# Second x chunk as plain rows, transposed on TensorE, and all of B in 128-row loads

## The chip, the cores and the metric

One core of a Trainium2 chip runs the kernel. The metric is the device time of one execution in microseconds (us), and lower is better. Every execution quoted here was classed as fast. "The profile" is the trace of one execution and the page made from it; its times are us from the start of the span. The span is some 1.8 us shorter than the device time of the same execution.

## The reference, cut to what matters

Only the first half of part A is touched by the change and by the argument: `Bu`, the product of x with two matrices B (real and imaginary part), ahead of a recurrence along the sequence.

```python
x: (1, 2048, 1024) bf16          B_re, B_im, C_re, C_im: (1024, 1024) bf16
Bu = einsum("bld,pd->blp", x, B_bar)          # contraction over d = 1024
for t in range(2048): h = Lam_bar * h + Bu[:, t, :]     # done in 8 chunks of 256
y = 2 * einsum("blp,dp->bld", hseq, Cmat).real + x * Dskip
out = g * y + (1 - g) * (x + an 8-row update of a gated MLP)
```

The kernel's matmuls contract over the partitions, so x and B are both needed transposed, with d on the partitions. Two chunks of x (512 rows) are worked on together: for each of eight channel tiles of 128 channels, 8 matmuls with B_re and 8 with B_im.

## The kernel before

The loads at the top, all on SyncE's queue but for one, and the opening of the work. `dma_start_transpose` loads and transposes in the DMA; `s1u` is one group of 8 matmuls (tile, B_re or B_im, chunks k0 to k1); `s1e` evicts a tile from PSUM on ScalarE; `warm` runs matmuls whose result nobody uses.

```python
x0r = const.tile([P, BPC, D], BF16, ...)                 # BPC = 2 tiles of 128 rows: chunk 0
for tl in range(BPC):
    (nc.scalar if tl else nc.sync).dma_start(x0r[:, tl, :], x2d[tl*P:(tl+1)*P, :])
load_B(0, 0, 1)                                          # B_re, channel tile 0, transposed
...                                                      # three tiny loads on ScalarE's queue
load_xT(1)                                               # chunk 1 of x, transposed, 256 rows
load_B(1, 0, 1)                                          # B_im, channel tile 0
for c0, c1 in ((1, 2), (2, 3), (3, 4), (4, 6), (6, 8)):
    for pl in range(2):
        load_B(pl, c0, c1)
load_X(1)                                                # chunks 2 and 3, then C, ...
...
warm(14)
for tl in range(BPC):                                    # chunk 0: 8 transposes a tile, then copies
    xq = ps_s2.tile([P, KD, P], BF16, name="xq", tag="zps")
    for dc in range(KD):
        nc.tensor.transpose(xq[:, dc, :], x0r[:, tl, dc*P:(dc+1)*P], ident[:])
    for h, copy in enumerate((nc.vector.tensor_copy, nc.scalar.copy)):
        copy(out=X[0][:, hs, tl*P:(tl+1)*P], in_=xq[:, hs, :])
warm(2)
...                                                      # tables: VectorE makes arguments, ScalarE sines
warm(1)
s1u(0, 0, 0, 0, 1)                                       # tile 0, B_re, chunk 0
warm(2)
s1u(0, 0, 0, 1, 2)                                       # tile 0, B_re, chunk 1
s1u(0, 0, 1, 0, 2)                                       # tile 0, B_im, both chunks
s1e(0, 0)
...                                                      # two tiny transposes (vb_ps), then
s1(0, 1)                                                 # tile 1: 16 matmuls of 512 columns
```

## Time and profile before

| | before |
|---|---|
| time, three timed runs | 247.49 us median (247.4 to 248.19) |
| span of the profiled execution | 246.1 us (device time 247.9) |
| TensorE busy | 240.6 us, 98% |
| VectorE, ScalarE busy | 92%, 48% |
| last wait of TensorE for a load | until 23.61 us |

Read it from the last row: TensorE is never without work after 23.61 us, so the end is fixed by when that stretch begins. The prediction shows the lines themselves.

### The profile page before, as it was taken

Reading aid. Unit: us, or ns where it says so; the run is one execution under the profiler, and the core shown is the slowest. Engines: PE = TensorE matmul, PEld = TensorE weight load, DVE = VectorE, ACT = ScalarE, POOL = GpSimd, SP = SyncE. Lnnn points to the kernel's source line nnn. Section 1 sums busy time; section 2 is a strip of 40 time slices with the busy share of each in tenths; the row PEclk is TensorE's granted clock in tenths of the full one; section 3 lists DMA queues with packets and bytes.
Section 4 is the critical chain, followed back from the end, with each engine's and each line's share of the span. In section 5 each row is a group of like instructions: output and inputs, shape, how many; then the busy total and the mean of one; then the engine's idle time right before and its main releaser. Section 6 shows DMA issues by size and latency. Waiting matters only on the chain.

```text
span 246.1 us, 3533 instructions
## 1 busy us (share of the span) xinstructions
PE 240.6 (98%) x1381; PEld 112.2 (46%) x1381; DVE 226.2 (92%) x230; ACT 119.3 (48%) x206; POOL 26.8 (11%) x47
## 2 busy tenths in 40 slices
PE   8998999999999999999999999999999999999994
PEld 5443444444444444444444444444444444446453
DVE  1799999999999999999999999999999999999932
ACT  3699973333462572223355462235267445456421
POOL 4000000000000301620002040100100211110210
PEclk9999999999999999999999999999999999999999
DMA  7899999999760450666257979778599999962052
GB/s 195 194 149 226 230 244 273 202 239 284 236 181 0 106 153 0 134 125 224 77 188 218 351 226 338 237 224 314 184 390 286 363 306 296 89 142 37 3 133 82
DMA packets 65313, 48.48 MB, mean 197 GB/s; under 512 B 50560, under 2 KB 52224, under 8 KB 65296
## 3 DMA queue, kind: packets, MB, share of 16 engines
q1 hardware_dynamic: 59968, 37.20, 58.1%
q0 software_dynamic: 3264, 7.38, 14.3%
q10 hardware_dynamic: 2064, 3.68, 4.1%
q8 instruction: 11, 0.18, 0.3%
q14 instruction: 6, 0.05, 0.1%
HBM read 27.55 MB, written 8.40 MB: 146 GB/s over the span
## 4 chain that ended last, share of the span: by engine, by line
PE 89%; SPq 7%; DMA 2%; issue 0%; DVE 0%
PE zps L767 42%; PE vps L271 39%; SPq L80 6%; PE zps L783 3%; PE pgu L659 3%; DMA BT<-in_A_B_im_dram 2%; PE y L671 1%; SPq L92 1%; PE zr L485 1%; DVE ot L788 0%; SPq L77 0%; PE xselT_ps L572 0%; PE zs_ps L588 0%; PE zt L492 0%; PE fl_ps L535 0%
## 5 line engine op out<-in xcount | busy, mean ns | idle before, releaser
L271 PE MATMUL vps<-X,BT 128*128 128x512 bf16 (+1 forms) x520 | 112.6, 376 | 1.2 <-DMA BT<-in_A_B_im_dram 0.9
L767 PE MATMUL zps<-CT,H 128*128 128x512 bf16 x480 | 105.0, 379 | 0.0
L271 PEld LDWEIGHTS <-BT 128*128 128x128 bf16 x520 | 50.1, 98 | 61.7 <-DMA BT<-in_A_B_im_dram 1.7
L767 PEld LDWEIGHTS <-H 128*128 128x128 bf16 x480 | 46.5, 98 | 56.6 <-issue 1.3
L278 ACT CAST V<-vps 128x512 bf16<-128x512 f32 x64 | 34.3, 588 | 58.6 <-PE vps L271 58.6
L308 DVE TENSOR_TENSOR_SCAN U<-d,U 128x2048 bf16<-128x2048 f32 (+2 forms) x22 | 62.0, 2860 | 0.6
L772 ACT ACTIVATE ot<-zps,gcol 128x512 bf16<-128x512 f32 x30 | 20.6, 686 | 46.3 <-PE zps L767 46.3
L741 ACT CAST zps<-xd 128x512 f32<-128x512 bf16 (+1 forms) x29 | 16.6, 576 | 3.6 <-ACT xt L728 3.3
L297 DVE TENSOR_TENSOR U<-V,T2tab 128x4096 bf16<-128x4096 bf16 (+2 forms) x11 | 16.6, 1511 | 0.7 <-ACT V L278 0.2
L298 DVE TENSOR_TENSOR V<-V,nTi 128x4096 bf16<-128x4096 bf16 (+2 forms) x11 | 16.7, 1516 | 0.5
L299 DVE TENSOR_TENSOR U<-U,V 128x4096 bf16<-128x4096 bf16 (+2 forms) x11 | 16.7, 1516 | 0.4
L793 POOL DMA_DIRECT2D out_dram<-ot x14 | 12.9, 923 | 32.5 <-ACT ot L772 30.4
L333 DVE TENSOR_TENSOR U<-U,S2tab 128x4096 bf16<-128x4096 bf16 x7 | 16.0, 2292 | 0.2
L335 DVE TENSOR_TENSOR H<-H,U 128x4096 bf16<-128x4096 bf16 x7 | 16.0, 2292 | 0.2
L728 ACT ACTIVATE xt<-xt,omgcol 128x1024 bf16<-128x1024 bf16 x14 | 16.0, 1144 | 0.0
L331 DVE TENSOR_TENSOR H<-U,Ctab 128x4096 bf16<-128x4096 bf16 x7 | 16.0, 2284 | 0.0
L705 POOL DMA_DIRECT2D xt<-in_A_x_dram x12 | 7.1, 594 | 80.9 <-DMA out_dram<-xt 42.9
L366 DVE TENSOR_TENSOR_SCAN U<-D,U 128x1024 bf16<-128x1024 f32 x4 | 8.9, 2279 | 0.1
L723 DVE TENSOR_TENSOR xd<-xt,Dbc 128x1024 bf16<-128x1024 bf16 x14 | 9.0, 683 | 0.0
L659 PE MATMUL pgu<-wgu,xsel 128*32 128x448 bf16 x128 | 7.2, 355 | 0.0
L783 PE MATMUL zps<-CT,H 128*128 128x256 bf16 (+1 forms) x48 | 7.1, 308 | 0.0
L718 POOL DMA_DIRECT2D out_dram<-xt x2 | 1.5, 752 | 49.2 <-DVE xt L717 49.2
(152 smaller groups left out, 127.6 us busy)
## 6 DMA issues: line engine op xcount, KB each, us to landing
wgu<-in_B_w_gate_dram SPq DMA_DIRECT2D x16, 448.0 KB, 3.5
wgu<-in_B_w_up_dram SPq DMA_DIRECT2D x16, 448.0 KB, 6.1
out_dram<-ot POOLq DMA_DIRECT2D x14, 256.0 KB, 6.0
wdb<-in_B_w_down_dram SPq DMA_DIRECT2D x7, 512.0 KB, 10.6
xt<-in_A_x_dram POOLq DMA_DIRECT2D x12, 256.0 KB, 4.3
out_dram<-xt ACTq DMA_DIRECT2D x12, 256.0 KB, 5.2
wd<-in_B_w_down_dram SPq DMA_DIRECT2D x5, 512.0 KB, 7.8
xt<-in_A_x_dram SPq DMA_DIRECT2D x4, 256.0 KB, 4.1
```

The lines of the kernel that those rows point to most:

```text
L271: nc.tensor.matmul(o, lhsT=BT[pl][:, dc, ct * P:(ct + 1) * P], rhs=X[m][:, dc, k0 * LC:k1 * LC], start=(dc == 0), stop=(dc == KD - 1))
L278: nc.scalar.copy(out=V[k][:, :, ct, :], in_=vp[m, ct][:, :, kk, :])
L297: nc.vector.tensor_tensor(out=u, in0=v, in1=T2tab[:, :, c0:c1, :], op=ALU.mult)
L298: nc.vector.tensor_tensor(out=v, in0=v, in1=bc(nTi, c0, c1), op=ALU.mult)
L299: nc.vector.tensor_tensor(out=u, in0=u, in1=V[k][:, ::-1, c0:c1, :], op=ALU.add)
L308: nc.vector.tensor_tensor_scan(out=fl, data0=d0[:, c0:c1, :].rearrange("p c t -> p (c t)"), data1=fl, initial=0.0, op0=ALU.mult, op1=ALU.add)
L331: nc.vector.tensor_tensor(out=h, in0=g, in1=bc(Ctab, c0, c1), op=ALU.mult)
L333: nc.vector.tensor_tensor(out=g, in0=g, in1=S2tab[:, :, c0:c1, :], op=ALU.mult)
L335: nc.vector.tensor_tensor(out=h, in0=h, in1=G[k][:, ::-1, c0:c1, :], op=ALU.add)
L741: nc.scalar.copy(out=z[:], in_=xd[b][:, d_:d_ + w])
L767: nc.tensor.matmul(zps[:], lhsT=H[k][:, pl, ct, tl * P:(tl + 1) * P], rhs=CT[pl][:, ct, dsl], start=(fresh and ct == 0 and pl == 0), stop= ...
L772: nc.scalar.activation(out=ots[b][:, dsl], in_=zps[:], func=ACT.Copy, scale=gcol[:, b:b + 1])
```

## The change

Its intent: take 2.6 us of issue out of SyncE's queue ahead of B by loading chunk 1 of x as plain rows and transposing it on TensorE, and let each tile of B come as early as it can by loading all of B in 128-row pieces. The helpers' new places are cut.

```diff
-    x0r = const.tile([P, BPC, D], BF16, name="x0r", tag="XP2")
+    x0r = const.tile([P, 2 * BPC, D], BF16, name="x0r", tag="XP2")
...
-    load_xT(1)
+    for tl in range(BPC, 2 * BPC):
+        nc.sync.dma_start(x0r[:, tl, :], x2d[tl * P:(tl + 1) * P, :])
     load_B(1, 0, 1)
-    for c0, c1 in ((1, 2), (2, 3), (3, 4), (4, 6), (6, 8)):
+    for c0, c1 in ((c, c + 1) for c in range(1, NCT)):
...
-        for h, copy in enumerate((nc.vector.tensor_copy, nc.scalar.copy)):
+        for h, copy in enumerate((nc.vector.tensor_copy if tl < BPC else nc.scalar.copy, nc.scalar.copy)):
...
+    warm(1)
+    s1u(0, 0, 0, 0, 1)
+    for tl in range(BPC, 2 * BPC):
+        x_tile(tl)
...
-    warm(1)
-    s1u(0, 0, 0, 0, 1)
-    warm(2)
-    s1u(0, 0, 0, 1, 2)
-    s1u(0, 0, 1, 0, 2)
+    s1u(0, 0, 1, 0, 1)
+    for pl in range(2):
+        s1u(0, 0, pl, 1, 2)
```

More of the change, by code (lines that the diff above doesn't have):

```diff
@@ L155, with x_tile @@
     vec = small.tile([P, 3, NCT], F32, name="vec")
-    for tl in range(BPC):
+    def x_tile(tl):
         xq = ps_s2.tile([P, KD, P], BF16, name="xq", tag="zps")
@@ L159 @@
             nc.tensor.transpose(xq[:, dc, :], x0r[:, tl, dc * P:(dc + 1) * P], ident[:])
-        for h, copy in enumerate((nc.vector.tensor_copy, nc.scalar.copy)):
+        for h, copy in enumerate((nc.vector.tensor_copy if tl < BPC else nc.scalar.copy, nc.scalar.copy)):
             hs = slice(h * KD // 2, (h + 1) * KD // 2)
             copy(out=X[0][:, hs, tl * P:(tl + 1) * P], in_=xq[:, hs, :])
+    for tl in range(BPC):
+        x_tile(tl)
     warm(2)
@@ L188, with s1u @@
     nc.scalar.activation(out=rdec[:], in_=are[:], func=ACT.Exp)
+    vp = {}
+    def s1u(m, ct, pl, k0, k1):
+        if (m, ct) not in vp:
+            vp[m, ct] = ps_s1.tile([P, 2, 2, LC], F32, name="vps", tag="vps")
+        o = vp[m, ct][:, pl, k0:k1, :].rearrange("p k t -> p (k t)")
+        for dc in range(KD):
+            nc.tensor.matmul(o, lhsT=BT[pl][:, dc, ct * P:(ct + 1) * P], rhs=X[m][:, dc, k0 * LC:k1 * LC], start=(dc == 0), stop=(dc == KD - 1))
+    warm(1)
+    s1u(0, 0, 0, 0, 1)
+    for tl in range(BPC, 2 * BPC):
+        x_tile(tl)
     Ctab = const.tile([P, NCT, LC], BF16, name="Ctab")
@@ L262 @@
     H = {}
-    vp = {}
-    def s1u(m, ct, pl, k0, k1):
-        if (m, ct) not in vp:
-            vp[m, ct] = ps_s1.tile([P, 2, 2, LC], F32, name="vps", tag="vps")
-        o = vp[m, ct][:, pl, k0:k1, :].rearrange("p k t -> p (k t)")
-        for dc in range(KD):
-            nc.tensor.matmul(o, lhsT=BT[pl][:, dc, ct * P:(ct + 1) * P], rhs=X[m][:, dc, k0 * LC:k1 * LC], start=(dc == 0), stop=(dc == KD - 1))
     def s1e(m, ct):
```

## The prediction

> **What bounds the kernel now.** I read the page's summary first, then the chain that ended last in order of time, then TensorE's waits, then the first 24 us engine by engine.
>
> ```profile
> PE 240.6 (98%) x1381; PEld 112.2 (46%) x1381; DVE 226.2 (92%) x230; ACT 119.3 (48%) x206; POOL 26.8 (11%) x47
> ...
> PE 89%; SPq 7%; DMA 2%; issue 0%; DVE 0%
> ```
>
> TensorE is busy for 98% of the span and makes up 89% of the chain; the other 9% (SyncE's issues and one transfer) is all ahead of 24 us. The chain, in order (start, length, what):
>
> ```profile
> 14.68 3.56 SPq L80
> 18.24 0.04 issue
> 18.29 5.27 DMA BT<-in_A_B_im_dram
> 23.56 0.05 issue
> 23.61 36.43 PE vps L271 x168
> ```
>
> The last thing TensorE waits for is the 256-row load of B_im for channel tiles 4 and 5, landed at 23.56. From 23.61 the chain is matmul after matmul to 242.9, so **the end is 23.61 plus a fixed 222.5 us**. Only what moves the matmuls at 23.61 can move the end. TensorE's own waits (total us, times, longest) say how much is lost there:
>
> ```profile
> PE vps L271 <- DMA BT<-in_A_B_im_dram: 0.9, 2, 0.7
> PE vps L271 <- DMA X<-in_A_x_dram: 0.2, 1, 0.2
> ```
>
> and its order of time (start, length, group) says where:
>
> ```profile
> 4.11 1.07 PE L159 MATMUL xq<-ident,x0r 128*128 128x128 bf16 x16
> ...
> 5.93 1.05 PE L271 MATMUL vps<-X,BT 128*128 128x256 bf16 x8
> 6.82 0.38 PE L152 MATMUL wps<-wt 128*128 128x256 bf16 x2
> 7.44 1.03 PE L271 MATMUL vps<-X,BT 128*128 128x256 bf16 x8 [0.24 <-DMA X<-in_A_x_dram]
> 8.65 1.90 PE L271 MATMUL vps<-X,BT 128*128 128x512 bf16 x8 [0.18 <-DMA BT<-in_A_B_im_dram]
> 10.48 0.20 PE L436 MATMUL vb_ps<-ident,vrow 8*128 8x8 bf16 x2
> 10.62 12.26 PE L271 MATMUL vps<-X,BT 128*128 128x512 bf16 x56
> 23.61 0.61 PE L271 MATMUL vps<-X,BT 128*128 128x512 bf16 x2 [0.73 <-DMA BT<-in_A_B_im_dram]
> ```
>
> The group at 10.62 is 56 matmuls (tiles 1, 2, 3 and half of 4) one every 0.216 us, without a hole; then 0.73 us of nothing. Two places can thus give time: the start of tile 1 (10.62) and the hole of 0.73.
>
> **What the Trainium skill says.** "TensorE: Matmul & The Clock Gate", Part 4 (PE-mode transpose): a TensorE transpose takes about 390 ns alone or 275 ns in one kernel, and its result lies in PSUM, so a copy has to follow. The trace agrees on the copy, but pipelined the 16 transposes stand one every 56 ns (1.07 us with the last one's latency). The same page, Part 1 (engine queue depths): ScalarE works strictly in order; ScalarE's row here does too, and my main doubt rests on it. "DMA: Bandwidth & Descriptors", "Issuing engines are not separate DMA queues": issue time is usually small beside the transfer. The trace disagrees for transposing loads: SyncE spends 1.31 us on 128 rows (256 KB) and 2.60 us on 256 rows, but 0.39 us on 128 plain rows. The same page, HWDGE ordering: each DMA engine takes descriptors in ring order, so the new rows stand behind B's first tile, not beside it.
>
> **The change part by part.**
>
> SyncE: the transposing load of x's second chunk (2.60 us of issue, 2.57 to 5.17) becomes two plain ones (2 x 0.39, plus 0.05 between issues, 0.88 in all). Every later issue is 1.76 us earlier. The four B loads of 256 rows become eight of 1.31: 0.0 to 0.2 more per pair than an unimpeded 2.60, so B_re tile 4 is issued at 14.68 - 1.76 = 12.92 and B_im tile 4 at 12.92 + 1.35 = 14.3, instead of in an instruction that ran from 18.29 to 20.71. With the 3.4 to 5.3 us that B loads took from issue to landing, it lands by 17.7 to 19.6; TensorE needs it near 23. **The hole of 0.73 goes**, with over 3 us to spare. Tiles 5, 6 and 7 follow at 2.7 us a pair against a need of 3.45 us a pair, and x's third and fourth chunks are still issued about 1.5 us earlier than before.
>
> TensorE: added are 16 transposes x 56 ns = 0.9 us, and the 8 matmuls of 512 columns become 16 of 256 (16 x 0.108 = 1.72 for 8 x 0.216 = 1.73: nothing). Removed are two warm-ups (0.2) and the waits 0.24 and 0.18. Step by step, as an estimate from these rows: B_re tile 0 lands at 5.9 as before, first half-group 5.93 to 6.79. Rows issued at 2.57 and 3.01 land near 6.3 and 6.8 (the transposed chunk, the same bytes in the same place, landed at 7.44 with its issue done only at 5.17). Transposes 6.79 to 7.69. B_im tile 0, issued at 3.45 in place of 5.21, lands near 7.9; its half-group runs 7.9 to 8.8. The other two half-groups need the copies.
>
> ScalarE: added are four copies, all in order. The same copies are in the trace before at 0.59 us latency and about 0.47 us from one start to the next. First one when the first eight transposes are done, 6.79 + 0.66 = 7.45 (the 0.66 is 4.11 to 4.77 before); starts 7.47, 7.94, 8.41, 8.88, end 9.46. TensorE starts chunk 1 when the third copy is done (9.0), its fifth matmul when the fourth is (9.5), so the two half-groups end at 9.95 and 10.8, two small transposes follow, and tile 1 starts at **10.95 against 10.62: 0.33 later**. From there 56 matmuls take 12.08: 23.03 in place of 23.61, a gain of **0.58 us**.
>
> The copies also push the table load behind them. Before:
>
> ```profile
> 6.94 1.28 ACT L223 ACT_TABLE_LOAD   x1
> 10.01 1.06 ACT L223 ACTIVATE nTi<-tf 128x1024 bf16<-128x1024 f32 x1 [1.78 <-DVE tf L212]
> ...
> 12.46 1.05 ACT L278 CAST V<-vps 128x512 bf16<-128x512 f32 x2
> ```
>
> Of the 1.78 us of slack, loading from 9.42 to 10.7 eats all and 0.7 more. ScalarE is without a gap from 10.01 to 25.4, so each eviction comes 0.7 later: tile 0 ends at 14.2, tile 1 (16.01 to 17.07 before) at 17.8. There are two accumulators, so tile 2 needs the first (TensorE is there at 14.40) and tile 3 the second (17.86). Both fit, with 0.2 and 0.1 us. I take off 0.08 for one of them missing: 0.5 us, **247.49 - 0.5 = 247.0**.
>
> **The rivals.** (1) *ScalarE takes over the wait.* The margins of 0.2 and 0.1 are thinner than my estimates of landings: rows or copies later by 0.4 make TensorE stop ahead of tile 2 or 3, each us of delay giving one us back. For it: the gapless ScalarE row. Against: it catches up before tile 5. It would give 247.2 to 247.6. (2) *The hole was all, and the start costs nothing*: rows land early, the ScalarE delay is small, tile 1 starts at 10.5: gain 0.8 to 1.0, 246.5. (3) *VectorE becomes the bound.* It is 92% busy and practically gapless from 6.4, and everything of it after the second table moves 0.7 later while TensorE comes 0.5 earlier. Against: its results are early; H of chunk 1 is done at 75.3 and used from 79.3, H of the last half-chunk at 232.2 and used from 235.8. A shift of 1.2 fits in 3.6, so no time. (4) *Smaller B loads starve TensorE*: 256 KB per 1.35 us is 194 GB/s against 512 KB per 3.45 us used, 152. Not unless a stall like that of the 3.56 us issue repeats, for which there are now 3 us. (5) The clock drops in the wait for the copies: the hole is under 0.5 us, so hardly; it would cost 1 to 2 us.
>
> **Range and chances.** Everything at stake is the 1.15 us that TensorE waits between 5.9 and 23.6 (0.24 + 0.18 + 0.73, 0.5% of the time), plus what new stalls can add. The best case is about 246.4. The worst of the plausible ones (rival 1 full, with a landing late by 1 us) is 248.0, and before itself ranges from 247.4 to 248.19. So 246.4 to 247.9 for 8 in 10; a change of 2% (5 us) needs something that no view shows.
>
> **What would show it.** Right: no wait on B after tile 1; B_im tile 4 landed before 20; 16 more transposes from about 6.8; four ScalarE copies from about 7.5 and the table load after them; tile 1 near 10.95; an unbroken TensorE from there; the group that started at 23.61 near 23.0. Wrong: TensorE waiting for an eviction before tile 2 or 3 (rival 1), a DMA wait on B or x further on (rival 4), a wait for H (rival 3), or a granted clock under 1.0 near 9 us (rival 5).

## The result, and the profile after

The changed kernel took **248.37 us** (median of 6, 247.86 to 248.49) against 247.49 (median of 6 in the same rounds, 247.4 to 248.7). The ratio is 1.0021, 95% interval 0.9999 to 1.0042: the same within 2%. Ratios here are the mean time of one kernel's fast runs over that of the other's of the same rounds, so not quite the ratio of the medians. A gain of 0.5 us was predicted, and the medians show a loss of 0.9.

The wait for B is gone, as predicted. Of the chain that ended last, by engine, the page of the changed kernel says

```profile
PE 97%; issue 1%; ACT 1%; DVE 0%
```

where SyncE's issues and a transfer held 9% before. TensorE waits for no load of B after tile 0. But the stretch without a hole begins late. TensorE's timeline of the changed kernel (start, length, group):

```profile
4.15 1.86 PE L161 MATMUL xq<-ident,x0r 128*128 128x128 bf16 x16
...
6.53 1.22 PE L202 MATMUL vps<-X,BT 128*128 128x256 bf16 x8
7.58 1.06 PE L161 MATMUL xq<-ident,x0r 128*128 128x128 bf16 x16
8.66 3.14 PE L202 MATMUL vps<-X,BT 128*128 128x256 bf16 x24
11.73 0.20 PE L445 MATMUL vb_ps<-ident,vrow 8*128 8x8 bf16 x2
12.09 38.15 PE L202 MATMUL vps<-X,BT 128*128 128x512 bf16 x173 [0.16 <-PE vb_ps L445]
```

The two tiny transposes `vb_ps` stand directly ahead of tile 1 and serve as its mark below: the records of tile 1's first matmul are sometimes missing, these two are not. They start at 11.73, against 10.48 before and 10.81 by the prediction's sum (its 10.95 for tile 1, less the 0.14 between the two marks before). The 16 transposes of chunk 0 take 1.86 us here and took 1.07 before, though the same instructions stand ahead of them in both kernels.

ScalarE's timeline of the changed kernel:

```profile
8.22 2.05 ACT L164 COPY X<-xq 128x512 bf16<-128x512 bf16 x4 [0.50 <-PE xq L161]
10.29 1.28 ACT L243 ACT_TABLE_LOAD   x1
11.59 1.06 ACT L243 ACTIVATE nTi<-tf 128x1024 bf16<-128x1024 f32 x1
```

The four copies and the table load behind them stand as foreseen, only 0.75 us later (the copies) and 0.87 us later (the load), and the first table entry comes at 11.59, 1.58 later than before. SyncE's timeline:

```profile
2.57 1.07 SPq L101 DMA_DIRECT2D x0r<-in_A_x_dram  x2
4.37 1.25 SPq L80 DMA_TRANSPOSE BT<-in_A_B_im_dram  x1
```

B_im tile 0 was issued at 4.37 and not at 3.45. SyncE's waits (total us, times, longest) say why:

```profile
SPq L80 <- DMA x0r<-in_A_x_dram: 0.7, 1, 0.7
```

Loads on SyncE's and ScalarE's queues take eight semaphores in turn, and in the changed kernel this load is the ninth: it waits until the very first load of x has landed.

More telling is when it landed. By the landing records B_im tile 0 came at 8.62, and at 8.60 before, though it was issued 0.84 us earlier; the prediction had 7.9. From 3 to 9 us the DMA share (the time of all packets over that of the 16 DMA engines) is 1.08 before and 1.11 after. That the transfers, and not the issues, set this landing is argued from that and from after_merge2 below, and not shown by an experiment of its own.

### The profile page after: what moved, and what is told of

Same layout as the page of the kernel before. It is cut to its first block, busy times and chain, and to the rows that moved or that the text cites. A ratio compares the mean times of both kernels' runs of the same rounds, so it can differ in the third digit from the quotient of the medians.

```text
span 246.7 us, 3563 instructions
## 1 busy us (share of the span) xinstructions
PE 240.4 (97%) x1379; PEld 114.6 (46%) x1403; DVE 225.9 (92%) x230; ACT 121.2 (49%) x210; POOL 26.8 (11%) x47
## 4 chain that ended last, share of the span: by engine, by line
PE 97%; issue 1%; ACT 1%; DVE 0%
PE vps L202 44%; PE zps L776 42%; PE zps L792 3%; PE pgu L668 3%; PE wps L153 1%; PE y L680 1%; PE xq L161 1%; PE zr L494 1%; ACT X L164 1%; DVE ot L797 0%; PE xselT_ps L581 0%; PE zs_ps L597 0%; PE zt L501 0%; DVE wt L130 0%; PE va_ps L171 0%
## 5 line engine op out<-in xcount | busy, mean ns | idle before, releaser
L202 PEld LDWEIGHTS <-BT 128*128 128x128 bf16 x528 | 51.1, 98 | 59.8 <-issue 1.3
```

Source lines behind the costliest of these rows:

```text
L202: nc.tensor.matmul(o, lhsT=BT[pl][:, dc, ct * P:(ct + 1) * P], rhs=X[m][:, dc, k0 * LC:k1 * LC], start=(dc == 0), stop=(dc == KD - 1))
```

## The experiments

Three theories. **A**: TensorE's clock is released at a moment that differs from execution to execution (the transposes stand 107 ns apart ahead of a trace's first clock record, at 5.85 us in the changed kernel, and 56 ns apart behind it, at 3.88 us before; an opening is called cold or warm by that), and a cold opening costs the changed kernel what the kernel before would have hidden in its wait for B. **B**, sharpened after the first runs to **C**: the new order of work makes tile 1 late whatever the clock, and the wait that the change removes is smaller in most executions than in the profiled one. A third: the smaller loads of B do the harm. Twelve kernels gave a result. One call of four was run by no chip, and the same four kernels were sent again under new labels (those with a 2 at the end). All twelve gave correct results. By the rule of 2% ten are the same as the kernel before and the two d kernels unclear, so what follows rests on the traces, one for each kernel, and on where the times lie.

| run | its own times, 6 each | ratio to before (95%) | first 16 transposes | `vb_ps` at |
|---|---|---|---|---|
| before_again | 247.89 (247.16 to 249.55) | 1.0012 (0.997 to 1.0055) | 1.07 | 10.51 |
| after_again | 248.25 (247.85 to 248.55) | 1.0025 (0.9991 to 1.0059) | 1.23 | 11.42 |
| b_only | 247.68 (247.51 to 247.89) | 1.0 (0.9967 to 1.0033) | 1.89 | 10.88 |
| x_only | 248.01 (247.76 to 248.43) | 1.0015 (0.9982 to 1.0049) | 1.89 | 11.82 |
| d_before2 | 252.43 (251.62 to 253.66) | 1.0197 (1.016 to 1.0233) | 1.05 | 15.05 |
| d_after2 | 252.49 (252.25 to 253.83) | 1.0194 (1.0162 to 1.0227) | 1.05 | 15.93 |
| after_rot2 | 248.09 (247.51 to 248.24) | 1.0003 (0.9976 to 1.0031) | 1.89 | 11.80 |
| after_merge2 | 248.59 (248.49 to 248.97) | 1.0034 (1.0007 to 1.0061) | 1.89 | 11.79 |
| after_dve | 248.47 (248.19 to 248.92) | 1.0037 (1.0018 to 1.0057) | 1.45 | 10.95 |
| after_merge_dve | 249.44 (248.99 to 249.71) | 1.0071 (1.0052 to 1.009) | 1.88 | 11.86 |
| b_only_rot | 247.25 (247.11 to 247.34) | 0.9985 (0.9967 to 1.0002) | 1.89 | 10.74 |
| after_merge_dve_rot | 248.47 (248.06 to 248.69) | 1.0036 (1.0017 to 1.0054) | 1.07 | 10.85 |

Each group of four ran on one chip beside 11 runs of the kernel before: 247.27 median (246.94 to 249.29) with the first four, 247.89 (246.99 to 249.17) with the next, 247.58 (246.99 to 248.59) with the last.

### The two kernels again

No edit.

> The kernel before, unchanged: how far two equal kernels differ, and a second trace of it. Theory A (TensorE's clock is released at a moment that varies from execution to execution, and the changed kernel's opening was cold in its profile, 1.86 us for the first 16 transposes against 1.07): the kernel before hardly cares, because a late tile 1 is absorbed in its wait for B_im, so 247.4 to 247.7, ratio 0.998 to 1.002, whatever the first 16 transposes took. Theory B (the ScalarE copies and the added transposes cost more than the wait that they remove, whatever the clock): the same.

> The changed kernel, unchanged, for a second trace. Theory A: its time follows the release of the clock: if the first 16 transposes take about 1.07 us, tile 1 starts near 11.0 us and the profiled span is near 245.6; if they take about 1.86, tile 1 starts near 12.1 and the span is near 246.7. Timed runs spread over 247.0 to 248.6. Theory B: tile 1 starts at 12 or later in either case, and the times stay at 248.2 to 248.5.

The kernel before is not one time: its runs reach from 246.94 to 249.55, while the changed kernel keeps to 247.85 to 248.55 in twelve. In this second profile of the kernel before the wait for B_im was longer:

```profile
PE vps L271 <- DMA BT<-in_A_B_im_dram: 1.5, 2, 1.1
PE vps L271 <- DMA X<-in_A_x_dram: 0.3, 1, 0.3
```

That execution took 248.71, and the median of the six, 247.89, lies above the 247.4 to 247.7 expected. Of the 1.5, 0.39 stands at tile 0, and 0.22 of that is a matmul whose record is missing. Counted from the start of one matmul to the start of the next, less the usual 0.22, the holes behind tile 1 cost 0.89 us in the first profile and 1.65 in the second. Without them the two executions would have taken 247.0 and 247.1 us, which is where the shortest runs lie. So the hole comes and goes, and by these two traces it is what makes the kernel before spread. What goes with it can be watched in the DMA view of the first profile between 15 and 20 us, in 40 slices of 0.125 us (busy tenths, then what was moved):

```profile
DMA  7989948979999999919500000005999999999998
GB/s 172 225 166 150 86 92 63 84 131 285 289 251 258 397 246 49 68 37 27 2 0 8 6 10 10 8 10 125 293 295 285 287 285 295 293 293 291 289 194 197
```

For about 1.5 us around 17 to 18 us next to nothing moved. In the trace 256-byte packets of the transposing loads that started at 17.0 took 1.43 us there (18 ns is usual), and a single 16 KB packet of the queue called "instruction" had begun at 16.72. SyncE's 256-row issue at 14.68 lasted until it was over, 3.56 us, and B_im came late. In the second profile the packet began at 16.08 and the standstill was 2.4 us. All fourteen traces have such a packet, begun anywhere between 10.96 and 17.98, and beside it 256-byte packets of 1.2 to 2.4 us. That it causes the standstill is argued from this, and not shown: no run moves the packet by itself.

In after_again the opening was nearly warm (1.23 us), and TensorE ran so:

```profile
7.05 1.06 PE L161 MATMUL xq<-ident,x0r 128*128 128x128 bf16 x16
8.69 2.79 PE L202 MATMUL vps<-X,BT 128*128 128x256 bf16 x24 [0.58 <-DMA BT<-in_A_B_im_dram]
11.42 0.20 PE L445 MATMUL vb_ps<-ident,vrow 8*128 8x8 bf16 x2
```

Theory A wanted `vb_ps` near 10.9 and a span of 245.6 here; it is 11.42 and 246.4. The clock accounts for some 0.3 us (11.42 against 11.73 to 11.82 in the cold openings), not for 1. What holds TensorE is B_im tile 0, landed at 8.64: the kernel before has 8 matmuls of 512 columns to do after that landing (1.7 us), the changed one has 24 of 256 (2.6 us).

### Each half of the change alone

```diff
 b_only: the kernel before, with
-    for c0, c1 in ((1, 2), (2, 3), (3, 4), (4, 6), (6, 8)):
+    for c0, c1 in ((c, c + 1) for c in range(1, NCT)):
 x_only: the changed kernel, with the first of these two lines again
```

> The kernel before with all of B in 128-row loads and x's second chunk still loaded transposed. Theory A: the wait of 0.73 for B_im goes (issued near 16 instead of 18.3), nothing is added on TensorE or ScalarE; 246.7 with an early clock, up to 247.6 with a late one. Theory B: 246.8 always. A third theory (the 128-row loads themselves do the harm, as more issues): 248 or more, as the changed kernel.

> The changed kernel with B's last loads of 256 rows again. The x part alone makes each later issue 1.8 us earlier, so no wait for B_im either way. Theories A and B: as the changed kernel, 248.2 to 248.5 (A: 247 when the clock is early). The third theory (128-row loads do the harm): 247.2 or less.

The loads of B do no harm at tile 1: b_only lies within 0.4 us in six runs and has none of the long executions of the kernel before, with the same mean (ratio 1.0). Its trace has the standstill too (an issue of 2.17 us at 16.45), but only a wait for B_im tile 0, printed as 0.28 us, of which a missing record makes 0.22; the later tiles come in time. It was expected at 246.7 to 247.6 and missed that: its tile 1 was 0.4 late (B_im tile 0 was issued at 5.62 and not at 5.21), and its four added loads cost 0.25 us at the end of the kernel (see the closing waits). The x half makes tile 1 late: `vb_ps` at 11.82, 248.01 us (0.2 under the 248.2 to 248.5 expected, and the end of this kernel is 0.25 us shorter than the changed kernel's). TensorE waits for no load of B in x_only either: each half alone takes the hole away.

### The clock released in every execution

```diff
+    nc.vector.memset(wt0[:], 0.0)
+    nc.vector.memset(CT[0][:], 0.0)          # some 4 us
+    nc.vector.memset(x0r[:, :, 0:2], 0.0)    # the first loads wait for this
...
-    warm(14)
+    warm(32)
```

> The kernel before with all loads held back by some 4 us behind a long VectorE memset, and 32 warm-up matmuls in place of 14, so that TensorE's clock is released before the first transposes in every execution (16 transposes in about 1.1 us). All theories: 251 to 252, 4 us over the kernel before; it is only the partner of d_after. The spread from the varying wait for B stays.

> The changed kernel with the same delay and warm-ups. Theory A (the late clock is what costs): with the clock always released it is 0.5 us faster than d_before2, as predicted for the change. Theory C (a later tile 1 by the changed order of work whatever the clock: tile 1 at 11.5 against 10.6, plus 0.25 us in the closing waits, less the wait for B of 0.2 to 0.4): 0.6 to 1.0 us slower than d_before2, ratio 1.002 to 1.004.

With both openings warm the lines that decide are, for d_before2,

```profile
13.44 1.67 PE L273 MATMUL vps<-X,BT 128*128 128x512 bf16 x7 [0.43 <-DMA BT<-in_A_B_im_dram]
15.05 0.20 PE L438 MATMUL vb_ps<-ident,vrow 8*128 8x8 bf16 x2
```

and for d_after2

```profile
13.21 2.79 PE L204 MATMUL vps<-X,BT 128*128 128x256 bf16 x24 [0.67 <-DMA BT<-in_A_B_im_dram]
15.93 0.20 PE L447 MATMUL vb_ps<-ident,vrow 8*128 8x8 bf16 x2
```

B_im landed at 13.17 and at 13.16 (the first of d_before2's eight matmuls has no record, so its line starts 0.22 late), and the changed order is 0.88 us later at tile 1: 24 matmuls of 256 columns and 8 of 512 take 2.72 and 1.83 us from there to `vb_ps`, which is all of it. Theory A is out by these lines: it wanted tile 1 in its place once the clock was early, and the changed kernel 0.5 faster. The times alone would not settle it, with intervals of 0.3 to 0.4% either way. C's expectation for the time was missed as well: the means are equal (1.0194 and 1.0197), since three of six runs of d_before2 were long ones, 252.95 to 253.66. The other three were 251.62 to 251.91, below all of d_after2's (252.25 and up).

### The closing waits

After the last matmuls the changed kernel loses more. From the start of the last VectorE instruction to the end of the span it is 3.40 us, and 3.18 before. The chains' last lines, before and after (spans 246.1 and 246.7):

```profile
242.95 0.48 DVE ot L788
```

```profile
243.30 0.48 DVE ot L797
```

At the end SyncE checks the eight DMA semaphores in a fixed order, one every 0.06 us in the trace. The number of loads in the kernel decides which one the last store has got, and those behind it are checked after the store has landed.

```diff
 after_rot2: the changed kernel, behind the loads of xt on SyncE's queue
+    pad = small.tile([NCT, 6, 16], BF16, name="pad")
+    for i in range(6):
+        nc.sync.dma_start(pad[:, i, :], A_log_dt.rearrange("(c p) -> c p", p=P)[:, 0:16])
```

> The changed kernel with six tiny loads added on SyncE's queue where it is idle, so that the last store uses the last of the eight DMA semaphores in the order in which SyncE checks them at the end. Theory C: the end of the last matmul to the end of the span takes 3.72 us in the changed kernel and 3.46 in the kernel before; with the last semaphore last in order it is 3.3 to 3.4, so 0.3 to 0.4 us less than the changed kernel: 247.9. Without that mechanism: 248.3 as the changed kernel.

The expectation counted from the last matmul, 0.32 us earlier. From the last VectorE instruction the traces give:

```
checks behind the last store's    0 (after_rot2)  2 (x_only)  3 (before)  6 (after)  7 (after_merge2)
to the end of the span, us        3.01            3.15        3.18        3.40       3.45
```

That is 0.06 us a check, and the other nine traces lie on the same line: 2.99 and 3.00 with no check (b_only_rot, after_merge_dve_rot), 3.18 with three, 3.40 with six, 3.43 and 3.46 with seven (b_only, after_merge_dve). So **0.2 us of the loss is the number of loads taken modulo 8**, and it comes from the four loads that the B half adds, not from the x half. The time, 248.09, came down less than the expected 247.9; its profiled opening was cold, with tile 1 as late as ever.

### What makes tile 1 late

```diff
 after_merge2: the changed kernel, with one load fewer
-    for tl in range(BPC, 2 * BPC):
-        nc.sync.dma_start(x0r[:, tl, :], x2d[tl * P:(tl + 1) * P, :])
+    nc.sync.dma_start(x0r[:, BPC:2*BPC, :], x2d[BPC*P:2*BPC*P, :].rearrange("(t p) d -> p t d", p=P))
 after_dve: the changed kernel, with half of the added copies on VectorE
-        for h, copy in enumerate((nc.vector.tensor_copy if tl < BPC else nc.scalar.copy, nc.scalar.copy)):
+        for h, copy in enumerate((nc.vector.tensor_copy, nc.scalar.copy)):
 after_merge_dve: both
 after_merge_dve_rot: both, and seven tiny loads
```

> The changed kernel with the two plain loads of x as one load of 256 rows. In the changed kernel B_im tile 0 was issued at 4.4 us, not at 3.45, because its semaphore was that of the very first load (0.7 us of wait for x0r). With one load fewer it waits for none: issue near 3.3. If B_im tile 0 then lands up to 0.8 earlier, its half-group moves, but the copies on ScalarE (done near 9.3 and 9.8) hold the rest, so tile 1 comes at 11.2 in place of 11.5: 0.2 to 0.4 faster than the changed kernel. If the DMA engines are the limit, B_im lands at 8.7 as before and nothing is gained.

> The changed kernel with half of the four added copies on VectorE instead of all four on ScalarE. Theory C has two limits ahead of tile 1 in the changed kernel: B_im tile 0 landing at 8.7, and the last ScalarE copy at 9.75 (10.3 with a late clock), after which 12 to 24 half-width matmuls remain. The copies end some 0.5 earlier here, but B_im still lands at 8.7 and 24 matmuls x 0.109 = 2.6 follow it, so the two small transposes ahead of tile 1 start at 11.4 whatever the clock (11.4 to 11.8 in the changed kernel): 0 to 0.3 faster than the changed kernel, 248.1. Rival (VectorE's table work, pushed back 0.9, now comes too late for ScalarE): 248.5 or more.

> Both: one load for the two x tiles, and half of the copies on VectorE. Theory C: with neither limit tile 1 starts at 10.9 to 11.2 instead of 11.5 to 11.9, so about 0.5 faster than after_merge2 (248.6), less 0 in the closing waits (the last store uses the first semaphore in order, the worst place): 248.0 to 248.2. If the DMA engines rather than the semaphore set B_im's landing, it is as after_dve.

> The changed kernel with all three repairs. Theory C: after_merge_dve less 0.42 us in the closing waits: 247.6 to 247.8, near b_only, so that the x part of the change is worth nothing even when repaired. If it is 247.0 or less, the x part was a good idea badly carried out.

Without the semaphore wait B_im tile 0 was issued at 3.21, 1.16 us earlier than in the changed kernel, and landed at 8.37, 0.25 earlier; in after_merge_dve it was issued at 3.23 and landed at 9.09. So the semaphore wait is real, but it is not what made B_im late. In after_merge2 nothing waited for B_im any more. Tile 1 stood at 11.79 all the same: the copies on ScalarE held it.

```profile
9.89 1.96 PE L201 MATMUL vps<-X,BT 128*128 128x256 bf16 x16 [0.33 <-ACT X L163]
11.79 0.20 PE L444 MATMUL vb_ps<-ident,vrow 8*128 8x8 bf16 x2
```

The time even rose (248.59, where 0.2 to 0.4 less than the changed kernel was expected), with the worst place in the closing waits. With half of the copies on VectorE tile 1 came early at last, `vb_ps` at 10.95, and still the time was 248.47: the rival named in the expectation came true, and not the 248.1. (B_im landed at 8.18 in this execution and at 8.64 in after_again, from issues 0.1 us apart; part of the early tile 1 is that.) TensorE and ScalarE of after_dve show what took over:

```profile
15.34 44.95 PE L202 MATMUL vps<-X,BT 128*128 128x512 bf16 x203 [0.63 <-ACT V L289]
```

```profile
11.79 1.06 ACT L243 ACTIVATE nTi<-tf 128x1024 bf16<-128x1024 f32 x1 [1.11 <-DVE tf L232]
...
14.23 1.05 ACT L289 CAST V<-vps 128x512 bf16<-128x512 f32 x2
```

The copies push VectorE's table arguments (`tf`) back, the table comes at 11.79, and the eviction of tile 0 behind it ends at 15.28; tile 2 needs that accumulator. TensorE gained 0.5 us (10.95 against 11.42 in after_again) and lost 0.63, or 0.8 from start to start. Both repairs together did the same (a wait of 0.66 in after_merge_dve, 0.75 in after_merge_dve_rot), so both expectations for them were missed by 0.7 us or more. In after_merge_dve the one load of x also came late and TensorE waited 0.50 us for it; why all six of its runs are some 1 us above after_merge_dve_rot's, when the closing waits account for 0.46, stays open. In after_merge_dve_rot, with a warm opening and no wait for B_im or for the copies, `vb_ps` came at 10.85, 0.37 after the kernel before: about the 0.33 of the prediction, but then tile 2 waits. The opening is a net of chains of nearly equal length: x to TensorE, B to TensorE, copies and tables to the first evictions. Work added to any of them comes out at tile 1 or at tile 2.

### A version that keeps the good half

```diff
 b_only_rot: b_only, and
+    pad = small.tile([NCT, 7, 16], BF16, name="pad")
+    for i in range(7):
+        nc.sync.dma_start(pad[:, i, :], A_log_dt.rearrange("(c p) -> c p", p=P)[:, 0:16])
```

> The kernel before with all of B in 128-row loads, and seven tiny loads so that the last store has the last semaphore in order. Theory C: b_only was 247.68 with a closing stretch of 3.72 us after the last matmul; here 3.34, so 247.3; and without the slow executions of the kernel before (6 of 6 within 0.4 us), so its mean is 0.4 to 0.7 below that of the kernel before, ratio 0.997 to 0.999.

247.25 us, with six runs between 247.11 and 247.34, as expected: 1.2 us or more under the changed versions on the same chip and 0.3 under the median of the kernel before. The ratio, 0.9985 (0.9967 to 1.0002), just fails to be clear of 1. TensorE of that execution, though its opening was cold:

```profile
10.74 0.20 PE L436 MATMUL vb_ps<-ident,vrow 8*128 8x8 bf16 x2
10.87 48.74 PE L271 MATMUL vps<-X,BT 128*128 128x512 bf16 x220
```

Tile 1 near the old place and no hole behind it: the change's gain without the x half's cost. The repaired x half ends with the same place in the closing waits (after_merge_dve_rot), and is 1.2 us longer.

## Why the prediction was wrong

The class (within 2%) was right, the number was not: 247.0 with a range of 246.4 to 247.9, and 248.37 came. By its own steps:

- **"The hole of 0.73 goes": right, but credited in full.** The hole is a matter of the execution. From start to start it cost 0.89 us in the profiled one, and the prediction's sum credits that (23.61 less 10.62 and 12.08 is 0.91). The profiled one took 247.9 us against a median of 247.49, so by an estimate from these the median holds a hole of some 0.5 us. Runs near 247.0 have next to none, those near 249 have 2. The term was too big by 0.4 us.
- **"Tile 1 starts at 10.95 against 10.62: 0.33 later": the step that failed.** Measured by `vb_ps` it is 0.9 to 1.1 later with a clock alike: 11.42 against 10.48 and 10.51 in warm openings, 11.73 to 11.82 against 10.74 (b_only_rot) in cold ones, 0.88 in the pair with the forced clock. The term under it that failed is "B_im tile 0, issued at 3.45 in place of 5.21, lands near 7.9". It was issued at 4.37, after 0.7 us of wait for a semaphore, and landed at 8.62, as late as before (8.60); even from an issue at 3.21 it landed at 8.37. The prediction let an earlier issue carry the landing with it. (The rows of x themselves landed at 6.24 and 7.10, near the 6.3 and 6.8 foreseen and behind B_re tile 0, at 5.80.) In the warm openings 2.7 us of half-width matmuls then stand between this landing and `vb_ps`, where the kernel before has 1.83. When the clock came late, the copies on ScalarE were the longer way (a wait of 0.23 us for them in after_rot2, 0.33 in x_only). And the prediction's "nothing" for splitting 8 matmuls of 512 columns into 16 of 256 held for the matmuls alone: more of them now stand behind the landing.
- **The closing waits**: no step foresaw them. 3.40 against 3.18, 0.2 us.
- The sum closes. From the profiled execution before to the one after: 247.90, less 0.89 for the hole, and 1.25 for tile 1 (some 0.3 of it the cold opening) and 0.21 for the end, is 248.47, the time of the changed kernel's profiled run. The prediction had 0.91 less and 0.41 more (0.33 and 0.08). That the median loses 0.9 and the profiled pair 0.57 is the hole's usual size again.
- **ScalarE's slack (rival 1)**: in the changed kernel itself no eviction held TensorE, as the main line said. The rival came true as soon as tile 1 was made early (after_dve, 0.63 us).
- **The clock (rival 5)**: said to matter only in a wait for the copies. It matters from the start: the first 16 transposes took anything from 1.05 to 1.89 us over the traces. It moves tile 1 by some 0.3 us in either kernel (10.74 against 10.48, 11.73 to 11.82 against 11.42) and is not the difference between the two.
- **VectorE and later loads (rivals 3 and 4)**: no wait for H or for a load of B or x was seen behind tile 0, as predicted. But the stall that rival 4 named did come (an issue of 3.14 us at 11.30): B_im tile 4 was issued at 17.19 and landed at 21.00, not at 14.3 and before 20. TensorE came to it near 24 (56 matmuls of 0.216 us behind tile 1's start at 11.9), so it cost nothing.

## What to carry to other kernels

Before you credit a change with a wait, compare the profiled execution's own time with the median: a wait that varies must enter with its usual size, and at times what it buys is less spread rather than a better median. In an opening where several chains end within half a microsecond, ask of each landing how much work stands behind it in the new order; taking the wait from one chain brings out the next. An earlier issue need not be an earlier landing: here 0.84 us at the issue were worth nothing at the landing. Count DMAs modulo the number of their semaphores: which early load a new one has to wait for, and which semaphore the last store gets.

## What the Trainium skill lacked or had wrong

- "TensorE: Matmul & The Clock Gate", Part 1, puts the release of the clock some 4 us into sustained work, give or take 0.5 us from run to run. Here the clock records begin between 3.8 and 7.1 us, with the first matmul always at 1.06: 2.7 to 6.0 us into the work, a spread of 3.3 us over fourteen traces. Part 4 of that page says that transposes do not bring the clock to its full rate; no run here tests that, since other matmuls go ahead of them in each. How they run once it is released it should add: here 56 ns apart, and 107 ns before.
- "Runtime: NRT & Kernel Launch", "Instruction fetch mechanics", has the fetch in 16 KiB blocks by a DMA queue, and calls its cost mostly hidden. The traces agree on the 16 KB packets, but those at 11 to 18 us stood beside 1.2 to 2.4 us in which transposing loads hardly moved. What such a fetch does to other queues the page doesn't say, and these runs show only that the two fall together.
- No page that I found has the closing checks: 0.06 us for each DMA semaphore checked after that of the last store, 0.44 us between the best and the worst place.
